# Seeds of a long convolution: phases that stay in PSUM, and sizes as eleven Exps on ScalarE

## The chip, the cores and the metric

One core of a Trainium2 chip runs the whole program. The metric is the device time of one execution in microseconds (us), the median of several runs. PE is the tensor engine (PEld its weight loads), DVE the vector engine, ACT the scalar engine, POOL the GpSimd engine, and SP issues the DMAs.

## The reference

Two independent blocks are written side by side into the output. Block B is softmax attention over 2048 positions with 16 heads of 28. Block A is a long convolution whose kernel is a sum of 256 complex exponentials for each of 448 channels:

```python
dt = jnp.exp(log_dt)
A = -jnp.exp(log_A_real) + 1j * A_imag
C = (C_real + 1j * C_imag) * dt[:, None]
P = jnp.exp((A * dt[:, None])[:, :, None] * pos[None, None, :])
K = 2.0 * jnp.einsum("dn,dnl->dl", C, P).real
y = irfft(rfft(u, 2L) * rfft(K, 2L))[:L] + u * D_skip
```

What matters here is P, the powers of z = exp(A dt) up to position 2047.

## The kernel before, in words

The kernel has two stages. The first projects x to q, k and v: 48 blocks of twelve matmuls each, in float32 split into a high and a low part, whose results leave PSUM through an ACT copy (the high part, hl or vst) and a DVE subtraction (the low part). PE has three PSUM tiles for these blocks, named pm. A block's hl goes to DRAM by a put on SP's queue, and the loads khat<-k and qhat<-q fetch it back. The first stage ends with the row maxima of the first 512 queries (mx, rl), which need those loads. The second stage runs attention and the convolution together, in a written order, up to the end.

The change is in the *seeds*, which run beside the projections. For eight groups of channels (seed 0 to 7), `seeds(o)` makes z to the powers 1, 2, 4, ..., 1024 (LV = 11 powers) for 112 exponents on each of 128 partitions, and from these the small tables that the second stage expands. Its steps are:

- `exp_a` and `times_dt` (ACT, nat): Exp of the decay parameters, and products with dt.
- `turn` (PE): eight transposes into the PSUM tile pn of the seed. Its part 0 is then the real part of A dt, part 1 the phase in turns, parts 2 and 3 are C.
- `phases` (DVE): reduces the phase to within half a turn in three small operations of 128x112 (round, subtract, clamp), and multiplies it with the eleven powers of two (pw) to r, 128x1232. On POOL it multiplies the real part with the same powers to mg, 128x1232.
- `reduce` (DVE): takes off whole turns, two operations of 128x1232.
- `sines` (ACT): sine, absolute value and cosine of 128x1232. `sizes` (ACT): Exp of mg, 128x1232.
- The rest (gz, sg, qhat, px on POOL, DVE and ACT) multiplies sizes with sines and cosines and puts the tables into DRAM. `fa`, `fb`, `e_base` and `g_base` read mg.

r, sn and mg are the three parts of one SBUF tile, tri, of which there are two. In groups of the profile "ACT tri<-tri" therefore holds sines, absolute values and the Exp of sizes alike; "DVE tri<-tri,pw" is the multiply of r, "DVE tri<-tri 128x112" the clamp, "POOL tri<-tr,pw" the product of mg, and tr is an SBUF copy of the real part that POOL reads.

Exp and Sin need different function tables on ACT; a change between them is an instruction of its own, ACT_TABLE_LOAD.

The steps of a seed are laid out over slots, four slots from one seed to the next, and the projections are spread evenly over 37 slots. In this stage a scheduler then orders each engine's queue by its own costs (in the second stage the written order is kept), and each engine works through its queue strictly in that order. All instructions pass through one helper, so the profile names line 75 for all of them; they are told apart by their tiles.

Of the kernel before, what the change touches and what calls it, by code (L numbers as in the profile page):

```python
# [2 lines left out]

# [5 lines left out]
F32 = mybir.dt.float32  # L9
F32R = mybir.dt.float32r  # L10
I32 = mybir.dt.int32
AF = mybir.ActivationFunctionType
ALU = mybir.AluOpType
# [42 lines left out]
LV = 11  # L56
# [4 lines left out]
MAGIC = 1.5 * 2 ** 23  # L61
TWO_PI = 6.283185
# [28 lines left out]
def body(ctx, tc, a, out):  # L91
# [5 lines left out]
    def pool(stack, name, bufs=1, space=None, side=None):  # L97
        kw = {} if space is None else {"space": space}
        if side:
            kw["side"] = side  # L100
        return stack.enter_context(tc.tile_pool(name=name, bufs=bufs, reuse_waits="tile", **kw))
# [110 lines left out]
    with ExitStack() as st:  # L212
        sst, xst, wst = ExitStack(), ExitStack(), ExitStack()
        t_p = pool(sst, "t_p")
        s_p = pool(sst, "s_p")
# [51 lines left out]
        half_pi = s_p.tile([128, 1], F32, name="half_pi")  # L267
# [42 lines left out]
        NH = BO * 16  # L310
        mul = lambda e, o_, x_, y_: e.tensor_tensor(o_, x_, y_, ALU.mult)

        def seeds(o):

            q = {}
            vec, pol, act = nc.vector, nc.gpsimd, nc.scalar
            lb = lambda v_: v_[:, None, :].to_broadcast([128, LV, NH])
            kb = pw2[:, :, None].to_broadcast([128, LV, NH])
            v = lambda t, k: t[:, k, :].rearrange("p (b h) -> p b h", h=16)
            vk = lambda t, k: t[:, k:k + 3, :].rearrange("p k (b h) -> p k b h", h=16)  # L320

            def exp_a():
                act.activation(q["nat"][:, 0, :], q["nat"][:, 0, :], AF.Exp)

            def times_dt(i):
                n, d = q["nat"][:, i, :], dt_all[:, i or 4, o:o + 1]
                act.activation(n, n, AF.Copy, scale=d)

            def turn():
                q["ps"] = ps = ps_n.tile([128, CQ], F32, name="pn")[:, :8 * PO].rearrange("p (a b h e) -> p a b h e", a=4, h=2, e=8)  # L330
                for i in range(4):
                    for h in range(2):
                        nc.tensor.transpose(ps[:, i, :, h, :], q["nat"][:, i, h * 128:(h + 1) * 128], ident[:PO, :PO])
                q["tr"] = s_p.tile([128, NH], F32, name="tr", bufs=2)
                act.activation(q["tr"], ps[:, 0].rearrange("p b h e -> p (b h e)"), AF.Copy)

            def phases():
                tri = t_p.tile([128, 3, LV, NH], F32, name="tri", bufs=2)
                q["r"], q["sn"], q["mg"] = r, sn, mg = tri[:, 0], tri[:, 1], tri[:, 2]
                t0, k0, im = sn[:, 0, :], sn[:, 1, :], q["ps"][:, 1].rearrange("p b h e -> p (b h e)")  # L340
                vec.tensor_scalar(k0, im, MAGIC, None, op0=ALU.add)
                vec.scalar_tensor_tensor(t0, k0, MAGIC, im, op0=ALU.subtract, op1=ALU.subtract)
                vec.tensor_scalar(t0, t0, 0.5, -0.5, op0=ALU.min, op1=ALU.max)
                mul(vec, r, lb(t0), kb)
                mul(pol, mg, lb(q["tr"]), kb)

            def reduce():
                vec.tensor_scalar(q["sn"], q["r"], MAGIC, MAGIC, op0=ALU.add, op1=ALU.subtract)
                vec.tensor_tensor(q["r"], q["sn"], q["r"], ALU.subtract)

            def sines():
                act.activation(q["sn"], q["r"], AF.Sin, scale=TWO_PI)
                act.activation(q["r"], q["r"], AF.Abs)
                act.activation(q["r"], q["r"], AF.Sin, scale=-TWO_PI, bias=half_pi)

            def sizes():
                act.activation(q["mg"], q["mg"], AF.Exp)

            def places():
                se = q_p.tile([128, HG, CQ], F32R, name="qhat", bufs=3).bitcast(F32).rearrange("p h q -> p (h q)")  # L360
# [40 lines left out]
            def factors(i, k, p_, n_):  # L401
                zz, mg = q["zz"], q["mg"]
                mul(vec, zz[:, i:i + 3, :, 0, :], vk(mg, k), vk(q["r"], k))
                mul(vec, zz[:, i:i + 3, :, p_, :], vk(mg, k), vk(q["sn"], k))
                for k in range(i, i + 3):
                    act.activation(zz[:, k, :, n_, :], zz[:, k, :, p_, :], AF.Copy, scale=-1.0)
# [20 lines left out]
            def load():  # L427
                if o not in nats:
                    load_nat(o)
                q["nat"] = nats.pop(o)  # L430
            dts = lambda *r: [lambda i=i: times_dt(i) for i in r]
            fa, fb = lambda: factors(0, 3, 2, 1), lambda: factors(3, 8, 1, 2)
            return [[load], [exp_a] + dts(1, 2, 3), dts(0), [turn], [phases], [reduce], [sines], [sizes, g_base],
                    [places, fa, e_base], [e3, g_first], [fb, e5, g_copies], [put_g], [put_e]]

        xh, xl = {}, {}
# [59 lines left out]
        for c in range(NQ):  # L496
# [4 lines left out]
            if c + 1 < NQ:  # L501
                jobs[1] = (lambda c, f: lambda: (load_x(c + 1), f())[1])(c, jobs[1])
            work += jobs
        stages = [seeds(o) for o in range(NO)]
        n_stage = SP * (NO - 1) + len(stages[0])
        slots = [[] for _ in range(n_stage)]
# [499 lines left out]
    for s in range(NS):  # L1006
# [25 lines left out]
        ps = []  # L1032
# [97 lines left out]
```

## Time and profile before

| | |
|---|---|
| timed runs | 1301.16, 1301.76, 1304.81 us; median 1301.76 |
| span of the profiled execution | 1301.1 us (1301.05 in the trace); its own device time is not listed apart from these runs |
| granted TensorE clock, mean | 0.978 |
| busy, share of the span | PE 94%, DVE 73%, ACT 73%, POOL 67% |

A group's line reads: line, engine, operation, output<-inputs, shape, count | busy us, mean ns | idle time of the engine just before, and what ended it. A piece of the chain of waits reads: start, length, what. A timeline line reads: start, length, engine, line, operation, tiles, shape, count, and in brackets the idle time before it. A row of a table of stretches has the busy time of PE, PEld, DVE, ACT and POOL, then the granted clock, the DMA engines' share and GB/s.

### The profile page before, as it was taken

What the parts mean: (1) busy time and instruction counts of PE and PEld (TensorE: products, weight loads), DVE (VectorE), ACT (ScalarE), POOL (GpSimd) and SP (SyncE); (2) the same over time, 40 slices, a digit from 0 to 9 for tenths busy, and PEclk for the clock granted to TensorE, in tenths of its full rate; (3) what the DMA queues carried; (4) which work ended last, traced back from release to release, by engine and by line L of the source; (5) the groups of instructions that cost most, each with busy time, mean ns of one, the idle gap of its engine ahead of it and who ended that gap; (6) DMA issues with size and microseconds to landing.
All of it is one profiled execution on the core that took longest, in us unless ns stands there. A gap on an engine that the chain in (4) does not pass through costs nothing.

```text
span 1301.1 us, 33177 instructions
## 1 busy us (share of the span) xinstructions
PE 1228.2 (94%) x12625; PEld 701.0 (54%) x12625; DVE 948.0 (73%) x2106; ACT 952.4 (73%) x2068; POOL 871.1 (67%) x736
## 2 busy tenths in 40 slices
PE   6878985899999999999999999999999999999997
PEld 5657763355555555555555555555555555544433
DVE  5887896987777887787788888888888655645111
ACT  4775763488888888888888888888887766756552
POOL 3676683298888878888869999998996212424421
PEclk9888997999999999999999999999999999999999
DMA  6677769835866555458644131733425453647656
GB/s 194 203 258 244 249 206 294 237 77 124 195 137 149 124 146 148 140 147 231 181 126 96 54 95 32 182 91 83 103 51 148 153 158 133 201 144 244 198 162 174
DMA packets 200088, 205.35 MB, mean 158 GB/s; under 512 B 95993, under 2 KB 158521, under 8 KB 197881
## 3 DMA queue, kind: packets, MB, share of 16 engines
q1 hardware_dynamic: 199928, 203.23, 56.2%
q8 instruction: 100, 1.64, 0.5%
q14 instruction: 60, 0.48, 0.1%
HBM read 120.73 MB, written 82.18 MB: 156 GB/s over the span
## 4 chain that ended last, share of the span: by engine, by line
PE 71%; DVE 10%; DMA 6%; POOL 5%; ACT 3%; issue 3%; SPq 0%; POOLq 0%; ACTq 0%; DVEq 0%
PE pm L75 40%; PE pss L75 16%; PE po L75 15%; DVE tri L75 2%; DVE mx L75 2%; POOL e L75 1%; POOL qhat L75 1%; DMA k<-hl 1%; ACT tri L75 1%; DVE qhat L75 1%; DVE sg L75 1%; DMA tri<-in_B_wqkv 1%; DVE px L75 1%; DMA khat<-k 1%; DMA ut<-in_A_u 1%
## 5 line engine op out<-in xcount | busy, mean ns | idle before, releaser
L75 ACT ACTIVATE p<-pss 128x512 f32<-128x512 f32 x1024 | 560.9, 609 | 111.6 <-PE pss L75 108.6
L75 PE MATMUL pss<-qhat,khat 128*128 128x512 f32 x1024 | 402.5, 399 | 1.5 <-ACT p L75 1.4
L75 DVE TENSOR_REDUCE mx<-pm 128x1 f32<-128x512 f32 x500 | 321.4, 684 | 109.2 <-PE pm L75 107.1
L75 PE MATMUL pm<-khat,qhat 128*128 128x512 f32 x749 | 326.3, 438 | 3.4 <-DVE mx L75 2.1
L75 POOL TENSOR_TENSOR e<-e,sdb 128x256 f32<-128x256 f32 x168 | 202.0, 1202 | 116.2 <-ACT e L75 61.2
L75 PE MATMUL po<-p,v 128*32 128x512 f32 x2048 | 269.1, 594 | 0.0
L75 POOL TENSOR_TENSOR e<-e,eu 128x256 f32<-128x256 f32 x168 | 248.4, 1478 | 13.2
L75 PEld LDWEIGHTS pm<-khat,qhat 128*128 128x128 f32 x749 | 141.0, 189 | 199.7 <-ACT p L75 47.8
L75 DVE CUSTOM_DVE_ANT_0 rl<-pm,rl 128x512 f32<-128x512 f32 x249 | 171.4, 688 | 65.2 <-ACT rl L75 61.5
L75 PEld LDWEIGHTS pss<-qhat,khat 128*128 128x128 f32 x1024 | 190.2, 188 | 45.7 <-issue 10.8
L75 POOL TENSOR_TENSOR eu<-e,sdb 128x256 f32<-128x256 f32 x168 | 202.2, 1203 | 0.0
L75 POOL TENSOR_TENSOR p<-pr,pr 64x448 f32<-64x448 f32 x64 | 73.3, 1145 | 158.5 <-PE pm L75 133.2
L75 ACT ACTIVATE rl<-pm 128x512 f32<-128x512 f32 x249 | 150.8, 606 | 20.4 <-PE pm L75 20.4
L75 DVE TENSOR_TENSOR g<-g,zg 128x128 f32<-128x128 f32 x392 | 162.1, 413 | 3.4
L75 PE MATMUL pm<-xh,khat 112*128 112x512 f32 x256 | 94.1, 451 | 23.2 <-DVE hl L75 11.1
L75 PE MATMUL pm<-kdif,qhat 128*128 128x512 f32 x249 | 100.5, 404 | 2.6 <-DMA v<-v 1.3
L75 DVE TENSOR_TENSOR zg<-g,zg 128x128 f32<-128x128 f32 x224 | 88.0, 393 | 5.0
L75 PEld LDWEIGHTS pm<-e,g 128*32 128x32 f32 x3584 | 57.2, 109 | 43.8 <-issue 16.1
L75 DVE TENSOR_TENSOR pr<-pm,ub 128x448 f32<-128x448 f32 x64 | 37.0, 619 | 56.4 <-PE pm L75 42.0
L75 PEld LDWEIGHTS pm<-xh,khat 112*128 112x128 f32 x256 | 54.2, 217 | 39.4 <-DVE hl L75 12.9
L75 PE MATMUL pm<-e,g 128*32 128x64 f32 x3584 | 73.0, 222 | 1.9 <-POOL e L75 1.9
L75 ACT ACTIVATE y<-pm 128x448 f32<-128x448 f32 x48 | 26.5, 553 | 58.2 <-PE pm L75 33.8
(134 smaller groups left out, 1470.3 us busy)
## 6 DMA issues: line engine op xcount, KB each, us to landing
sdb<-sd SPq DMA_DIRECT2D x56, 336.0 KB
khat<-k SPq DMA_DIRECT2D x64, 256.0 KB
qhat<-q SPq DMA_DIRECT2D x64, 256.0 KB
sd<-sg SPq DMA_DIRECT2D x8, 1456.0 KB
k<-hl SPq DMA_DIRECT2D x16, 512.0 KB
q<-hl SPq DMA_DIRECT2D x16, 512.0 KB
mw<-in_mw SPq DMA_DIRECT2D x16, 512.0 KB
sd<-qhat SPq DMA_DIRECT2D x8, 896.0 KB
```

The lines of the kernel that those rows point to most:

```text
L75: i = f(*args, **kw)
```

## The change

The copy tr and POOL's product are gone. The phase stays in PSUM through its three small operations (the first still writes its rounded copy to SBUF), and the multiply reads it from there. The sizes are eleven ACT instructions of 128x112, each Exp of the turned real part, read from PSUM, with the power of two as its scale. They stand right behind the phases in a seed's steps. A helper, `in_order`, tells the scheduler to keep those ACT steps that need a table (`exp_a`, `sizes`, `sines`) in the order in which they are written, over all seeds.

```diff
+        table = []
...
+            def in_order(f):
+                def call():
+                    with tc.issue_after(table[0]) if table else nullcontext():
+                        i = f()
+                    table[:] = [i.ins]
+                return call
...
-                q["tr"] = s_p.tile([128, NH], F32, name="tr", bufs=2)
-                act.activation(q["tr"], ps[:, 0].rearrange("p b h e -> p (b h e)"), AF.Copy)
...
-                t0, k0, im = sn[:, 0, :], sn[:, 1, :], q["ps"][:, 1].rearrange("p b h e -> p (b h e)")
-                vec.tensor_scalar(k0, im, MAGIC, None, op0=ALU.add)
-                vec.scalar_tensor_tensor(t0, k0, MAGIC, im, op0=ALU.subtract, op1=ALU.subtract)
+                k0, (tr, t0) = sn[:, 1, :], (q["ps"][:, i].rearrange("p b h e -> p (b h e)") for i in range(2))
+                vec.tensor_scalar(k0, t0, MAGIC, None, op0=ALU.add)
+                vec.scalar_tensor_tensor(t0, k0, MAGIC, t0, op0=ALU.subtract, op1=ALU.subtract)
                 vec.tensor_scalar(t0, t0, 0.5, -0.5, op0=ALU.min, op1=ALU.max)
                 mul(vec, r, lb(t0), kb)
-                mul(pol, mg, lb(q["tr"]), kb)
+                q["tr"] = tr
...
+            @in_order
+            def sizes():
+                return [act.activation(q["mg"][:, k, :], q["tr"], AF.Exp, scale=float(2 ** k)) for k in range(LV)][-1]
...
-            def sizes():
-                act.activation(q["mg"], q["mg"], AF.Exp)
...
-            return [[load], [exp_a] + dts(1, 2, 3), dts(0), [turn], [phases], [reduce], [sines], [sizes, g_base],
+            return [[load], [exp_a] + dts(1, 2, 3), dts(0), [turn], [phases, sizes], [reduce], [sines], [g_base],
```

More of the change, by code (lines that the diff above doesn't have):

```diff
@@ L1 @@
 import collections
-from contextlib import ExitStack
+from contextlib import ExitStack, nullcontext
 import concourse.bass as bass
@@ L320, in seeds @@
             vk = lambda t, k: t[:, k:k + 3, :].rearrange("p k (b h) -> p k b h", h=16)
+            def in_order(f):
[5 more added lines that the diff above has]
+            @in_order
             def exp_a():
-                act.activation(q["nat"][:, 0, :], q["nat"][:, 0, :], AF.Exp)
+                return act.activation(q["nat"][:, 0, :], q["nat"][:, 0, :], AF.Exp)
             def times_dt(i):
@@ L339, in phases @@
                 q["r"], q["sn"], q["mg"] = r, sn, mg = tri[:, 0], tri[:, 1], tri[:, 2]
-                t0, k0, im = sn[:, 0, :], sn[:, 1, :], q["ps"][:, 1].rearrange("p b h e -> p (b h e)")
-                vec.tensor_scalar(k0, im, MAGIC, None, op0=ALU.add)
-                vec.scalar_tensor_tensor(t0, k0, MAGIC, im, op0=ALU.subtract, op1=ALU.subtract)
+                k0, (tr, t0) = sn[:, 1, :], (q["ps"][:, i].rearrange("p b h e -> p (b h e)") for i in range(2))
+                vec.tensor_scalar(k0, t0, MAGIC, None, op0=ALU.add)
+                vec.scalar_tensor_tensor(t0, k0, MAGIC, t0, op0=ALU.subtract, op1=ALU.subtract)
                 vec.tensor_scalar(t0, t0, 0.5, -0.5, op0=ALU.min, op1=ALU.max)
                 mul(vec, r, lb(t0), kb)
-                mul(pol, mg, lb(q["tr"]), kb)
+                q["tr"] = tr
+            @in_order
+            def sizes():
+                return [act.activation(q["mg"][:, k, :], q["tr"], AF.Exp, scale=float(2 ** k)) for k in range(LV)][-1]
             def reduce():
@@ L349, in reduce @@
                 vec.tensor_tensor(q["r"], q["sn"], q["r"], ALU.subtract)
+            @in_order
             def sines():
@@ L353, in sines @@
                 act.activation(q["r"], q["r"], AF.Abs)
-                act.activation(q["r"], q["r"], AF.Sin, scale=-TWO_PI, bias=half_pi)
-            def sizes():
-                act.activation(q["mg"], q["mg"], AF.Exp)
+                return act.activation(q["r"], q["r"], AF.Sin, scale=-TWO_PI, bias=half_pi)
             def places():
```

## The prediction

> **What bounds the kernel now.** I read the page's chain of the whole span first, then a table of stretches, then the chain inside the stretch that the change touches.
>
> ```profile
> PE 71%; DVE 10%; DMA 6%; POOL 5%; ACT 3%; issue 3%; SPq 0%; POOLq 0%; ACTq 0%; DVEq 0%
> ```
>
> ```profile
> 28.00:191.00 163.00, 137.63 (x613) 111.04 (x611) 137.34 (x224) 116.86 (x232) 114.74 (x121) 0.91 0.70 235
> ...
> 196.60:215.00 18.40, 6.44 (x22) 4.85 (x20) 9.10 (x20) 4.75 (x10) 8.74 (x13) 0.69 1.04 294
> 216.00:247.00 31.00, 24.70 (x63) 11.72 (x61) 29.38 (x65) 9.24 (x16) 0.00 (x0) 0.93 1.00 288
> 260.00:1260.00 1000.00, 991.08 (x11443) 537.44 (x11442) 735.46 (x1707) 780.94 (x1732) 721.31 (x568) 1.00 0.51 136
> ```
>
> The columns are stretch, length, busy time of PE, PEld, DVE, ACT and POOL, granted clock, DMA share and GB/s. From 260 to 1260 us PE is busy for 991 of 1000 us, and the change has no instruction there. From 216 to 247 DVE's maxima are busy for 29.4 of 31 us. From 196.6 to 215 the DMA engines are full (1.04) with the loads that the maxima wait for. So whatever the change does to the seeds, between 28 and about 195 us, passes on to the end one for one: those three stretches only begin earlier or later. Within the seeds no engine is full: PE 137.6, DVE 137.3, ACT 116.9 and POOL 114.7 of 163 us. The limit there is a chain that changes engines, so I take its pieces (start, length, what):
>
> ```profile
> by line: DVE tri L75 16.8%; POOL qhat L75 10.7%; PE pm L75 10.3%; DVE sg L75 7.6%; DVE qhat L75 7.3%; ACT tri L75 6.6%; issue 6.5%; POOL tri L75 5.5%; DVE px L75 4.5%; DVE hl L75 3.7%; POOL x_e L75 2.9%; DMA sd<-qhat 2.5%; DMA v<-vst 2.2%;
> ...
> 46.92 1.77 DVE tri L75
> ...
> 77.07 3.41 POOL tri L75
> ...
> 116.00 6.54 PE pm L75 x24
> ...
> 124.41 1.98 DVE tri L75
> ...
> 143.78 2.96 DVE tri L75
> ...
> 160.97 2.28 DVE qhat L75
> ...
> 182.07 1.64 DVE tri L75
> ```
>
> DVE's work on tri (the phases) is the largest share, and POOL and DVE lines together hold more than half. The pieces of 1.6 to 3 us are the ones to explain, because the tiles in them are small.
>
> **What the change removes.** Groups, with count, busy time and mean ns:
>
> ```profile
> L75 ACT ACTIVATE tri<-tri 128x1232 f32<-128x1232 f32 x24 | 29.6, 1234 | 15.7 <-POOL tri L75 10.8 <-DVE tri L75 4.8
> L75 POOL TENSOR_TENSOR tri<-tr,pw 128x1232 f32<-128x1232 f32 x8 | 19.4, 2419 | 14.3 <-ACT tr L75 8.5 <-issue 5.8
> L75 ACT ACT_TABLE_LOAD x15 | 19.2, 1283 | 1.0 <-PEq L1120 0.7
> L75 DVE TENSOR_TENSOR tri<-tri,pw 128x1232 f32<-128x1232 f32 x8 | 15.1, 1886 | 0.1
> L75 DVE TENSOR_TENSOR hl<-pm,hl 128x512 fp32r<-128x512 f32 x16 | 11.0, 686 | 4.8 <-ACT hl L75 4.7
> L75 DVE TENSOR_TENSOR qhat<-qhat 128x112 f32<-128x112 f32 x16 | 10.1, 655 | 3.4 <-POOL qhat L75 3.4
> L75 DVE TENSOR_SCALAR tri<-tri 128x112 f32<-128x112 f32 x8 | 8.0, 1003 | 0.1
> L75 DVE TENSOR_TENSOR px<-pn,gz 128x224 f32<-128x224 f32 x16 | 6.4, 400 | 0.3
> L75 ACT ACTIVATE tr<-pn 128x112 f32<-128x112 f32 x8 | 2.2, 271 | 1.1 <-PE pn L75 0.9
> L75 DVE TENSOR_SCALAR tri<-pn 128x112 f32<-128x112 f32 x8 | 2.1, 267 | 0.2 <-ACT tr L75 0.2
> ```
>
> The clamp of the phases (tri<-tri, 128x112) takes 1003 ns on average, its neighbour from pn with as many elements 267. Two of its eight in order of time say why:
>
> ```profile
> 33.23 0.21 DVE L75 TENSOR_SCALAR tri<-tri 128x112 f32<-128x112 f32 x1
> ```
>
> ```profile
> 181.39 2.24 POOL L75 TENSOR_TENSOR tri<-tr,pw 128x1232 f32<-128x1232 f32 x1
> ...
> 181.95 1.76 DVE L75 TENSOR_SCALAR tri<-tri 128x112 f32<-128x112 f32 x1
> ```
>
> Alone it takes 0.21 us. At 181.95 it ends at 183.71, just as POOL's product does (183.63): DVE stood still behind POOL. The operations that have an operand in PSUM (hl, px) show nothing of the kind in their means.
>
> - *Clamp, in PSUM now.* The trace has no DVE instruction that writes PSUM of this size from PSUM. Its bounds are 0.21 and 1.00 us; I take the row from pn, 0.27. The three clamps on the chain give 1.50 + 1.71 + 1.37 = 4.6 us.
> - *Multiply to eleven powers, one operand in PSUM.* From 686 ns at 512 elements and 400 at 224, an element costs 0.99 ns, so 1232 take 1.40 us (bounds: that and today's 1.89). The one on the chain at 143.78 gives 2.96 - 1.40 = 1.6 us.
> - *POOL's product goes.* The multiply at 160.97 (qhat), held behind it, falls to its group's mean of 0.65: 1.6 us. At 77.07 it is itself on the chain. Late next there is DVE's multiply of the same seed:
>
> ```profile
> 76.08 2.29 DVE L75 TENSOR_TENSOR tri<-tri,pw 128x1232 f32<-128x1232 f32 x1
> ```
>
> ```profile
> 80.50 1.23 ACT L75 ACTIVATE tri<-tri 128x1232 f32<-128x1232 f32 x1 [2.79 <-POOL tri L75]
> ```
>
>   In the built program a seed's first Exp waits for that multiply, the last of DVE's four operations in the seed's PSUM tile. With 1.40 it ends at 77.48 instead of Exp's start at 80.50. That is 3.0 us earlier, less 0.7 by which the new Exps are longer (below): 2.3.
>
> Together 10.1 us of the chain. I count nine tenths, 9.0: paths beside it lie close, but they run over the same two engines, and off the chain DVE and POOL are released as well (eight clamps by 0.73 us, eight multiplies by 0.49, eight products of 2.42).
>
> **What it adds.** Eleven Exps of 128x112 from PSUM replace one of 128x1232 and the copy tr, in each of eight seeds. Bounds from rows: 11 x 0.271 = 2.98 us end to end, or overlapped as this row's six are:
>
> ```profile
> 195.35 1.22 ACT L75 ACTIVATE sg<-sg 128x112 f32<-128x112 f32 x6
> ```
>
> Six take 1.22, so one costs 0.20 us more and eleven some 0.27 + 10 x 0.18 = 2.0 (with 0.18 for the shorter single one). I take 2.0, nearest to the row that has them back to back. ACT gains 2.0 - 1.23 - 0.27 = 0.5 us a seed, 4 in all (12 by the other end). The order of the built program has 17 table loads in place of 15, another 2.6 us. So ACT gets 6.6 us more work and loses the 10.8 us that it waited for POOL's product. Bounds of what reaches the path: nothing, or all 6.6. ACT's tri is 6.6% of the chain, and only one Exp is on it, so I take a quarter: 1.6.
>
> [...]
>
> A table load is followed at once:
>
> ```profile
> 135.10 1.28 ACT L75 ACT_TABLE_LOAD   x1
> 136.40 0.42 ACT L75 ACTIVATE nat<-nat 56x256 f32<-56x256 f32 x1
> ```
>
> [...]
>
> **What it moves.** The last seed sets the tail, and there the order on ACT changes.
>
> ```profile
> 184.12 1.80 DVE L75 TENSOR_TENSOR tri<-tri,pw 128x1232 f32<-128x1232 f32 x1
> ...
> 190.76 1.23 ACT L75 ACTIVATE tri<-tri 128x1232 f32<-128x1232 f32 x1 [2.16 <-DVE tri L75]
> ...
> 194.00 0.69 DVE L75 TENSOR_TENSOR hl<-pm,hl 128x512 fp32r<-128x512 f32 x1 [0.57 <-ACT hl L75]
> ...
> 195.25 0.99 POOL L75 TENSOR_TENSOR tri<-tri 128x224 f32<-128x224 f32 x1 [2.20 <-ACT tri L75]
> ...
> 196.57 1.80 SPq L75 DMA_DIRECT2D khat<-k  x4
> ```
>
> Between sine and cosine stands the evacuation hl of a q block. Behind it wait PE for its PSUM tile and, on SP's queue, the put of q, then two loads of kdif, then khat<-k, which opens the full DMA stretch. Now hl ends 3.9 us after the sine starts. In the new order ACT does sine, absolute value and cosine first (3 x 1.23, as its tri group), two copies (0.27 each, as tr) and gz (0.4, as twice a copy's elements), 4.6 in all, and then hl; and DVE's half of hl stands behind an operation (0.4, as px) that waits for POOL's product of cosines: 4.6 + 0.1 + 1.0 + 0.4 + 0.7 = 6.8. So +2.9. From the multiply's end to the sine it is 190.76 - 185.92 = 4.8 now; then two table loads, Exps and an hl between them, 1.3 + 2.0 + 0.7 + 1.3 = 5.3: +0.5. Two px operations of seed 6 (0.4 each) go behind that multiply: -0.8. SP's own order from here on, and the bytes, are the same. The tail costs 2.6.
>
> **Sum:** -9.0 + 1.6 + 2.6 = -4.8. The profiled execution has a span of 1301.05 us; its own device time is not listed apart, and the timed runs start at 1301.16, so little lies around it. Against the span that is 1296.3; the median is 0.7 above it, which makes **1297.0**.
>
> **The rivals.**
>
> *The pair runs free (about 1292).* Everything that DVE loses counts: clamps 5.9, multiplies 3.9, the held qhat 1.6, and half of what the reductions lose today, 8 x (1.1 - 0.8) + 8 x (1.85 - 1.45):
>
> ```profile
> L75 DVE TENSOR_TENSOR tri<-tri 128x1232 f32<-128x1232 f32 x8 | 14.8, 1847 | 0.1
> ...
> L75 DVE TENSOR_SCALAR tri<-tri 128x1232 f32<-128x1232 f32 x8 | 8.8, 1098 | 0.1
> ```
>
> ```profile
> 127.89 0.81 DVE tri L75
> 128.72 1.45 DVE tri L75
> ```
>
> That is 14.2, so -14.2 + 1.6 + 2.6 = -10.0: 1291.8, and less where POOL's own 19.4 us count. For it: DVE and POOL hold the chain. Against: PE, ACT and the DMAs have stretches of their own in it.
>
> *The stall moves on (about 1301).* POOL keeps 95 of its 115 us, and now starts its other products earlier, beside DVE's reductions and sg products, which still have both operands in SBUF. Only the clamps' 4.6 are kept: -4.6 + 1.6 + 2.6 = -0.4, 1301.4. This is also the case in which the change does not do what it says.
>
> *The Exps hold up the evacuations (about 1312, slower).* The first Exp now waits at the head of ACT's queue for DVE's multiply; behind it stand the evacuations hl, vst and xh, and for these PE, which has three tiles: it can run two blocks, 6.54 us, before it stalls. The train is 1.28 + w + 2.0 + 0.42 (Exp of the next parameters) + 1.28 = 5.0 + w, so it decides from a wait w of 1.5 us on. The four waits for POOL's product averaged 10.8 / 4 = 2.7. With that in all eight seeds, and DVE's 0.7 for its half, PE loses 8 x 1.9 = 15 us: -4.8 + 15 = +10, 1312. Half of the seeds give 1304.5. Against: the wait is for an earlier operation than today's.
>
> **How the numbers follow.** A measurement of this kernel can tell about 0.3%, 3.9 us, from no change. I give the forecast (1293 to 1300) 0.45, the free pair 0.20, the moved stall 0.17 and the held evacuations 0.18. Faster by over 0.3% (below 1297.9): 0.31 of the forecast's 0.45 and the 0.20, 0.51. Within: 0.14 + 0.17 = 0.31. Slower: 0.18. The range 1289 to 1306 takes in the first three and the lower part of the last; 1293 to 1300 is the forecast's own.
>
> **What would show it.** Right: clamps near 0.27 us and multiplies near 1.4, ACT's wait for POOL tri gone, Exps about 0.18 us apart, the first khat<-k near 192, and all later stretches unchanged in length. Wrong: ACT waiting on DVE at the first Exps by more than 1.5 us each with PE's waits for hl rising above today's; clamps still near 1 us; or a shorter chain with khat<-k no earlier, which would put the error into the tail.

## The result, and the profile after

The changed kernel takes 1293.94 us, the median of four runs (1296.34, 1293.33, 1291.53, 1294.55), against 1303.28 of the kernel before beside it. The ratio is 0.9922, with a 95% interval of 0.9902 to 0.9942: 10.2 us faster (7.6 to 12.8). (The two medians differ by 9.3 us, which lies inside that interval; the expectations below name that figure.) The forecast was 4.8. The profiled execution is the slowest of the four: its span is 1294.3 us and its time 1296.34, so 2.0 us lie around the span. (The prediction took nearly nothing for that, for want of the number; the profiled execution of before then took some 1303.)

The chain of waits inside the seeds' stretch, 28 to 191 us, and then the table of stretches, both of the changed kernel. The two middle stretches are set 8 us earlier than those shown of before, as its loads and maxima begin earlier by that:

```profile
by line: PE pm L75 24.6%; ACT tri L75 11.4%; issue 7.4%; POOL qhat L75 6.6%; DVE tri L75 5.9%; DVE sg L75 5.6%; DVE qhat L75 4.9%; DMA q<-hl 3.8%; DVE px L75 3.7%; DVE hl L75 3.4%; POOL x_e L75 3.3%; POOL tri L75 3.0%; ACT L75 2.9%; PE pt L
```

```profile
28.00:191.00 163.00, 141.12 (x624) 115.20 (x624) 127.89 (x239) 129.83 (x322) 96.83 (x123) 0.88 0.72 245
...
188.50:207.00 18.50, 6.03 (x22) 4.49 (x20) 8.39 (x18) 2.83 (x7) 6.16 (x6) 0.68 1.04 292
...
208.00:239.00 31.00, 24.66 (x63) 11.59 (x61) 29.34 (x65) 9.30 (x16) 0.00 (x0) 0.94 1.01 287
260.00:1260.00 1000.00, 990.77 (x11448) 536.94 (x11446) 731.07 (x1697) 779.67 (x1730) 715.49 (x563) 1.00 0.51 137
```

In the chain of the seeds' stretch DVE's tri fell from 16.8% to 5.9%, and PE's pm, the projections, rose from 10.3% to 24.6%. The DMA stretch is as full as it was (1.04), the maxima as busy (29.3 of 31 us), and 260 to 1260 us unchanged. POOL has 18 us less work in the same 163 us, and ACT 13 more, in part because more of the stage falls into them (624 PE instructions for 613). The groups of the first 240 us:

```profile
L75 ACT ACT_TABLE_LOAD x17 | 21.8, 1283 | 4.8 <-DVE tri L75 3.9 <-PEq L1130 0.7
...
L75 DVE TENSOR_TENSOR sg<-tri 128x336 f32<-128x336 f32 x32 | 21.3, 680 | 10.5 <-ACT tri L75 10.5
...
L75 ACT ACTIVATE tri<-pn 128x112 f32<-128x112 f32 x88 | 15.2, 310 | 0.1
...
L75 DVE TENSOR_TENSOR tri<-tri 128x1232 f32<-128x1232 f32 x8 | 13.6, 1703 | 0.1
...
L75 DVE TENSOR_TENSOR tri<-pn,pw 128x1232 f32<-128x1232 f32 x8 | 11.4, 1429 | 0.0
...
L75 DVE TENSOR_TENSOR px<-qhat 128x112 f32<-128x112 f32 x16 | 8.5, 532 | 3.9 <-POOL qhat L75 3.7 <-issue 0.2
...
L75 DVE TENSOR_SCALAR tri<-tri 128x1232 f32<-128x1232 f32 x8 | 7.4, 930 | 0.0
L75 DVE TENSOR_TENSOR qhat<-qhat 128x112 f32<-128x112 f32 x16 | 7.2, 480 | 2.4 <-POOL qhat L75 2.4
...
L75 DVE TENSOR_SCALAR pn<-pn 128x112 f32<-128x112 f32 x8 | 2.2, 273 | 0.0
```

Clamps take 273 ns and multiplies 1429, as forecast (270 and 1400); the reductions and the qhat products became shorter too (1847, 1098 and 655 before); the products sg<-tri and px<-qhat hardly changed (684 and 504 before). ACT's waits of 10.8 us for POOL's product are gone; in their place a table load waited twice for DVE's multiply, 3.9 us in all.

The tail of the last seed, from the timeline, engine by engine:

```profile
171.30 1.42 DVE L75 TENSOR_TENSOR tri<-pn,pw 128x1232 f32<-128x1232 f32 x1
...
185.95 0.68 DVE L75 TENSOR_TENSOR hl<-pm,hl 128x512 fp32r<-128x512 f32 x1
```

```profile
174.09 1.83 ACT L75 ACTIVATE tri<-pn 128x112 f32<-128x112 f32 x11
...
177.80 1.23 ACT L75 ACTIVATE tri<-tri 128x1232 f32<-128x1232 f32 x1
...
182.85 0.39 ACT L75 ACTIVATE gz<-gz 128x224 f32<-128x224 f32 x1 [2.33 <-POOL gz L75]
...
184.36 0.57 ACT L75 ACTIVATE hl<-pm 128x512 fp32r<-128x512 f32 x1
```

```profile
188.50 1.98 SPq L75 DMA_DIRECT2D khat<-k  x4
```

The last seed's multiply ends at 172.72 (start and length) in place of 185.92: 13.2 us earlier. The first khat<-k is issued at 188.50 in place of 196.57, only 8.1 earlier. So the seeds gave more than forecast, and 5.1 us were given back between the two. Eleven Exps stand together in 1.83 us (forecast 2.0).

### The profile page after: what moved, and what is told of

Same layout as the page of the kernel before. It is cut to its first block, busy times and chain, and to the rows that moved or that the text cites. A ratio compares the mean times of both kernels' runs of the same rounds, so it can differ in the third digit from the quotient of the medians.

```text
span 1294.3 us, 33256 instructions
## 1 busy us (share of the span) xinstructions
PE 1228.1 (95%) x12625; PEld 703.1 (54%) x12625; DVE 933.2 (72%) x2106; ACT 956.6 (74%) x2142; POOL 847.0 (65%) x728
## 4 chain that ended last, share of the span: by engine, by line
PE 76%; DVE 9%; POOL 5%; ACT 4%; issue 3%; DMA 3%; SPq 0%; ACTq 0%; POOLq 0%; DVEq 0%
PE pm L75 43%; PE pss L75 16%; PE po L75 16%; DVE mx L75 2%; ACT tri L75 1%; POOL e L75 1%; DVE rl L75 1%; DMA khat<-k 1%; POOL qhat L75 1%; DVE tri L75 1%; DVE px L75 1%; DVE sg L75 1%; DVE qhat L75 1%; POOL p L75 1%; PE pt L75 1%
## 5 line engine op out<-in xcount | busy, mean ns | idle before, releaser
L75 POOL TENSOR_TENSOR e<-e,eu 128x256 f32<-128x256 f32 x168 | 248.1, 1477 | 13.2
L75 PEld LDWEIGHTS pss<-qhat,khat 128*128 128x128 f32 x1024 | 190.7, 189 | 45.7 <-issue 10.8
L75 PE MATMUL pm<-xh,khat 112*128 112x512 f32 x256 | 90.3, 434 | 14.1 <-DVE hl L75 7.1
```

The source lines that it names most:

```text
L75: i = f(*args, **kw)
```

## The experiments

Two theories stood against each other. *Release*: the gain is DVE and POOL set free, by PSUM operands that POOL doesn't hold (before, 267 ns for the rounding from pn and 1003 for the clamp in SBUF, of the same shape) and by the product that is gone. *Order*: the gain comes from the new order of ACT's functions, and the edits matter little. A scheduler orders this stage anew after every edit, so beside the ratio I read three points of each profiled execution: the end of the last seed's multiply, the first khat<-k, and the first copy rl of the maxima. *Tail* is from the first to the second, *loads* from the second to the third. The end follows the third within 3.8 us (span less first rl: 1085.4 to 1089.2 in all fourteen).

| kernel | multiply ends | tail | loads | span | ratio to before (95%) |
|---|---|---|---|---|---|
| before | 185.92 | 10.65 | 19.11 | 1301.1 | |
| after | 172.72 | 15.78 | 19.24 | 1294.3 | 0.9922 (0.9902 to 0.9942) |
| e1 phases in PSUM alone | 181.52 | 15.13 | 19.61 | 1302.0 | 1.0008 (0.9995 to 1.0022) |
| e2 Exps on ACT alone | 171.24 | 15.70 | 19.48 | 1292.5 | 0.9938 (0.9922 to 0.9953) |
| e3 changed, free order | 167.82 | 11.47 | 19.19 | 1286.5 | 0.9875 (0.9857 to 0.9893) |
| e4 new order alone | 186.27 | 15.86 | 19.18 | 1307.4 | 1.0049 (1.0033 to 1.0066) |
| e5 changed, product back | 179.18 | 15.76 | 19.43 | 1300.8 | 0.9993 (0.9983 to 1.0004) |
| e17 as e2, product back | 186.76 | 15.73 | 19.39 | 1310.7 | 1.0055 (1.0043 to 1.0068) |
| e16 changed, hl ahead | 169.32 | 13.64 | 19.55 | 1289.0 | 0.9908 (0.9893 to 0.9923) |
| e10 as e2, free order | 167.41 | 18.97 | 19.29 | 1292.8 | 0.9925 (0.9912 to 0.9937) |
| e18 changed, hl behind sine | 169.74 | 12.47 | 15.54 | 1286.9 | 0.9876 (0.9861 to 0.9891) |
| e19 as e1, hl behind sine | 183.72 | 12.53 | 15.99 | 1299.1 | 0.9966 (0.9952 to 0.9979) |
| e20 as e10, hl behind sine | 167.19 | 18.50 | 15.70 | 1289.2 | 0.9889 (0.9873 to 0.9906) |
| e8 changed, Exps twice | 182.49 | 11.36 | 19.13 | 1300.4 | 0.9983 (0.9975 to 0.9991) |

Each run of a batch was timed beside the kernel before on its chip. Differences between ratios below are given in us of 1304 (the median of before in the three batches was 1304.2 to 1304.75), with the two intervals added as squares.

### Halves and order (e1 to e4)

e1 starts from the kernel before:

```diff
-                t0, k0, im = sn[:, 0, :], sn[:, 1, :], q["ps"][:, 1].rearrange("p b h e -> p (b h e)")
-                vec.tensor_scalar(k0, im, MAGIC, None, op0=ALU.add)
-                vec.scalar_tensor_tensor(t0, k0, MAGIC, im, op0=ALU.subtract, op1=ALU.subtract)
+                k0, t0 = sn[:, 1, :], q["ps"][:, 1].rearrange("p b h e -> p (b h e)")
+                vec.tensor_scalar(k0, t0, MAGIC, None, op0=ALU.add)
+                vec.scalar_tensor_tensor(t0, k0, MAGIC, t0, op0=ALU.subtract, op1=ALU.subtract)
```

> Only the first half: phases stay in PSUM; the copy tr, POOL's product and the one Exp of 128x1232 stay as in the kernel before, and so does the free order of the functions (15 table loads). Release theory (DVE is freed where an operand is in PSUM, and POOL's product is a cost of its own): clamps 0.27 us and multiplies 1.4 us, ACT's wait for POOL tri still about 10 us, and 4 to 6 us of the 9.3 that the whole change gained, 1297 to 1299. If this half is all of it: 1294. Order theory (the gain is that of the new order of ACT's functions): no gain, 1302 to 1304.

e2 is the changed kernel with t0 in sn again (the diff of e1 turned round). e3 is the changed kernel without its three `@in_order`:

```diff
-            @in_order
             def sizes():
```

e4 is the kernel before with `in_order` on its three steps, and sizes moved behind the phases in the list of steps:

```diff
+            @in_order
             def sizes():
-                act.activation(q["mg"], q["mg"], AF.Exp)
+                return act.activation(q["mg"], q["mg"], AF.Exp)
...
-            return [[load], [exp_a] + dts(1, 2, 3), dts(0), [turn], [phases], [reduce], [sines], [sizes, g_base],
+            return [[load], [exp_a] + dts(1, 2, 3), dts(0), [turn], [phases, sizes], [reduce], [sines], [g_base],
```

> Only the second half: eleven Exps from PSUM and no product on POOL, in the new order, but the phases in SBUF as before. Release theory: the clamps were held behind just the product that is gone, so most of them fall to 0.2 to 0.4 us with operands in SBUF too, and the mean goes below 0.6; multiplies 1.4 to 1.9; total 1295 to 1298. If the place of the operands is what counts: clamps stay near 1.0, because POOL's other products take the place of the one removed, total 1299 to 1301. Order theory: 1294, whatever the clamps do.

> The changed kernel with the order of ACT's functions left free; 19 table loads in place of 17. Release theory: the gain stays but for the two loads, 2.6 us of ACT's time of which at most all is seen: 1294 to 1297. Order theory: the gain is gone, 1302 to 1304.

> The kernel before with the new order alone: the Exp of the powers is written right behind the phases and the functions keep that order (17 table loads in place of 15); phases in SBUF, POOL's product, one Exp of 128x1232. Release theory: no gain, and the two loads and the earlier wait for POOL's product cost up to some 5 us: 1303 to 1308. Order theory: 1294 to 1296.

The order theory falls: without the order the change gives 16.3 us in place of 10.2, and the order alone costs 6.4 (plus or minus 2.2), somewhat more than the 5 that the release theory allowed. Nearly all of that cost is in the tail: the multiply ends at 186.27 in e4 and at 185.92 before, the tail is 15.86 in place of 10.65.

In e1 the clamps and multiplies were as short as in the changed kernel:

```profile
L75 DVE TENSOR_TENSOR tri<-pn,pw 128x1232 f32<-128x1232 f32 x8 | 11.5, 1438 | 0.2
...
L75 DVE TENSOR_SCALAR pn<-pn 128x112 f32<-128x112 f32 x8 | 2.2, 272 | 0.1
```

The last multiply ended 4.4 us earlier, but nothing was left of it in the time. In e1's order ACT's evacuation hl stands behind the cosine, a table load and six copies sg, and the tail took 4.5 back:

```profile
189.18 1.29 ACT L75 ACTIVATE tri<-tri,half_pi 128x1232 f32<-128x1232 f32 x1
...
193.49 0.58 ACT L75 ACTIVATE hl<-pm 128x512 fp32r<-128x512 f32 x1
```

The time is the one that the order theory named (no gain), but not for its reason, and the release theory's 4 to 6 us did not arrive. e3, in turn, gained more than the release theory allowed (1287.92 for 1294 to 1297): its free order has hl directly behind the last sine, and a tail of 11.47.

e2 has no PSUM operands for the phases, and yet DVE is free:

```profile
L75 DVE TENSOR_TENSOR tri<-tri,pw 128x1232 f32<-128x1232 f32 x8 | 11.6, 1455 | 0.1
...
L75 DVE TENSOR_SCALAR tri<-tri 128x112 f32<-128x112 f32 x8 | 2.3, 283 | 0.1
```

283 ns a clamp and 1455 a multiply, where they had 1003 and 1886 before, and a time of 1296.13 us: as the release theory expected. So it was above all the one product of POOL, issued at the same moment, that held them (before, the three longest clamps, 1.77, 1.97 and 1.76 us, stood beside it, two more, of 0.86 and 1.02, beside a product x_e<-qhat), and once it is gone the place of the operands matters little: e2 and the changed kernel differ by 2.1 us, plus or minus 3.3.

### The product put back (e5 and e17)

```diff
-                k0, (tr, t0) = sn[:, 1, :], (q["ps"][:, i].rearrange("p b h e -> p (b h e)") for i in range(2))
+                k0, (tr, t0) = s_p.tile([128, NH], F32, name="k0", bufs=2), (q["ps"][:, i].rearrange("p b h e -> p (b h e)") for i in range(2))
...
+                junk = s_p.tile([128, LV, NH], mybir.dt.bfloat16, name="junk")
+                mul(pol, junk, lb(k0), kb)
```

Nothing reads junk. k0 gets a tile of its own, which the product reads. e5 is the changed kernel with this, e17 is e2 with it. In both kernels each queue is as in its twin (after, e2) but for these eight products, so that the scheduler has no part in the difference.

> The changed kernel with POOL's product of eleven powers put back, written to a tile that nothing reads (in 16 bits, for room), so that no engine waits for it; every engine's order is that of the changed kernel but for these eight instructions. Theory A (the product costs by POOL's time and by what it holds on DVE): clamps stay at 0.27 us as their operands are in PSUM, but reductions and qhat products on DVE get longer again and POOL's 19 us delay what follows; 5 us or more of the gain are lost, a ratio to the kernel before of 0.996 to 1.001. Theory B (the product cost by ACT's wait for it at the one Exp): nobody waits now, the ratio stays at 0.992 to 0.994.

> The run with the phases in SBUF and the Exps on ACT, with POOL's product put back in the same way, read by nobody; every engine's order is that of that run but for the eight products. Clamps should go back from 0.28 to some 1.0 us, held behind the product. Theory A: ratio to the kernel before 0.999 to 1.004, and the step from its twin without the product is larger than that of the pair with the phases in PSUM by 2 to 5 us, since here the clamps and multiplies are held too. Theory B: 0.994 to 0.996, though the clamps are long.

```profile
L75 DVE TENSOR_TENSOR sg<-tri 128x336 f32<-128x336 f32 x32 | 23.9, 759 | 10.1 <-ACT tri L75 10.1
...
L75 POOL TENSOR_TENSOR junk<-k,pw 128x1232 bf16<-128x1232 f32 x8 | 18.5, 2315 | 7.4 <-DVE k L75 7.4
...
L75 DVE TENSOR_TENSOR tri<-tri 128x1232 f32<-128x1232 f32 x8 | 14.8, 1854 | 0.1
...
L75 DVE TENSOR_TENSOR tri<-pn,pw 128x1232 f32<-128x1232 f32 x8 | 11.4, 1431 | 0.1
...
L75 DVE TENSOR_TENSOR px<-qhat 128x112 f32<-128x112 f32 x16 | 10.3, 646 | 4.0 <-POOL qhat L75 3.7 <-ACT sg L75 0.3
...
L75 DVE TENSOR_TENSOR qhat<-qhat 128x112 f32<-128x112 f32 x16 | 8.7, 574 | 2.2 <-POOL qhat L75 2.2
...
L75 DVE TENSOR_SCALAR tri<-tri 128x1232 f32<-128x1232 f32 x8 | 7.7, 962 | 0.0
...
L75 DVE TENSOR_SCALAR pn<-pn 128x112 f32<-128x112 f32 x8 | 2.2, 272 | 0.0
```

```profile
L75 DVE TENSOR_TENSOR tri<-tri,pw 128x1232 f32<-128x1232 f32 x8 | 16.0, 2001 | 0.1
...
L75 DVE TENSOR_SCALAR tri<-tri 128x112 f32<-128x112 f32 x8 | 10.3, 1283 | 0.1
```

Theory A holds in both (e17 lies a little above its range). The product that nobody waits for costs 9.3 us (plus or minus 2.9) with the phases in PSUM, nearly all that the change gained, and 15.3 (2.6) with them in SBUF. In e5 clamps (272) and multiplies (1431) are untouched by it, but the product now holds what stands beside them, DVE work that still has its operands in SBUF. In seed 3, e5 has, on POOL and on DVE,

```profile
96.34 2.25 POOL L75 TENSOR_TENSOR junk<-k,pw 128x1232 bf16<-128x1232 f32 x1 [0.25 <-DVE k L75]
```

```profile
96.65 2.18 DVE L75 TENSOR_TENSOR px<-qhat 128x112 f32<-128x112 f32 x1
```

and the changed kernel, for the same instruction,

```profile
96.63 0.37 DVE L75 TENSOR_TENSOR px<-qhat 128x112 f32<-128x112 f32 x1
```

That is 1.8 us, and the multiply of that seed ends 1.85 us later (100.64 for 98.79). Over all seeds sg<-tri, px<-qhat, the qhat products and the reductions get longer by 7.3 us: (759 - 680) x 32 + (646 - 532 + 574 - 480) x 16 + (1854 - 1703 + 962 - 930) x 8 ns. In e17 clamps (1283) and multiplies (2001) are held for 12.4 us more than in e2, sg<-tri (786 for 703) for 2.7 more, and px<-qhat (573 for 614) for 0.7 less: 14.4 in all. So 7.1 us more of holding cost some 6.0 (3.9) more, and the holding on DVE, 7.3 and 14.4 us, is nearly the whole of the two prices, 9.3 and 15.3. What is left for POOL's own time, 18.5 us ahead of the tables in its queue and 7.4 us in which it stands there waiting for k, is 2.0 and 0.9 us, not told from nothing. No run separates the two, and none shows that each us of holding reaches the end: in e1, which has another order, clamps, multiplies and these groups together are 10.1 us shorter than before the change, and the last multiply ends only 4.4 earlier.

Beside the same product the multiply takes 1431 ns with one operand in PSUM (e5) and 2001 with both in SBUF (e17), and px<-qhat above, with both in SBUF, 2.18 us in place of 0.37. By what POOL holds DVE, no run here shows.

### The tail (e16, e18, e19) and the free order (e10, e20)

e16 holds the last seed's absolute value, gz and cosine, and its negated factors, behind ACT's hl of the q block:

```diff
+                    hls.append(nc.scalar.activation(th, pp, AF.Copy).ins)
...
+                mark[:] = [hls[-2]]
+                with tc.issue_after(mark[0]):
+                    act.activation(q["r"], q["r"], AF.Abs)
```

> The changed kernel, in which the last seed's absolute value, gz and cosine are put behind ACT's evacuation hl of the q block (and so is DVE's half, two places earlier); the order of PE, POOL and SP is that of the changed kernel. Tail theory (the 5 us between the last multiply and the first khat<-k that the changed kernel gives back are ACT's order there): DVE's hl ends about 3 to 4 us earlier, first khat<-k near 185, ratio to the kernel before 0.989 to 0.990. Rival (the tail waits for something else, POOL's products or SP): khat<-k no earlier than 188, ratio 0.992.

The tail fell by 2.1 us in place of 3 to 4, and the ratio by 1.8 us (plus or minus 3.3, so not told from none). hl still waited, as the copies sg<-px of the seed before stood ahead of it, and these waited 3.27 us for DVE:

```profile
179.37 0.56 ACT L75 ACTIVATE sg<-px 128x112 f32<-128x112 f32 x2 [3.27 <-DVE sg L75]
179.73 0.63 ACT L75 ACTIVATE hl<-pm 128x512 fp32r<-128x512 f32 x1
```

e18 puts these copies behind hl as well. For that seed 6's `g_copies` and `put_g` had to be written later, which moved one more thing, its put sd<-sg on SP's queue, behind two loads qhat<-q and four khat<-k:

```diff
-                    [places, fa, e_base], [e3, g_first], [fb, e5, g_copies], [put_g], [put_e]]
+                    [places, fa, e_base], [e3, g_first], [fb, e5] + [g_copies] * (o != NO - 2),
+                    [put_g] * (o != NO - 2), ([g_copies, put_g] if o == NO - 2 else []) + [put_e]]
```

e19 and e20 make the same edit in e1 and in e10 (e10 is e2 without `@in_order`). In e16, e18, e19 and e20 the queues are those of their twins up to the last sine, but for two copies sg<-pn that e20 moves from before that sine to behind the cosine.

> The changed kernel with ACT's evacuation hl of the last q block directly behind the last seed's sine; absolute value, gz, cosine and the copies sg of the seed before come after it, and DVE's half is two places earlier than in the changed kernel. All else is in the order of the changed kernel. Tail theory: from the last multiply's end to the first khat<-k 12 to 13 us in place of 15.8, as DVE's half now waits for DVE's own queue alone; ratio to the kernel before 0.989 to 0.990. Rival (something else holds the tail): 15 us or more, ratio 0.991 to 0.993.

> The run with phases in PSUM alone, with the same tail as the last one: hl directly behind the last sine; the order before that is unchanged. If that run's 4.4 us at the last multiply were real and only the tail's order ate them: tail 11 to 13 us in place of 15.1, ratio to the kernel before 0.997 to 0.998 from 1.0008, 4 us faster than the kernel before. Rival (released clamps and multiplies are worth nothing, as the timed run says): 1.000 to 1.001.

> Exps on ACT in a free order of ACT's functions, phases in SBUF: the run with the free order without the first half of the change. If the place of the phases is worth the 2 us by which the two runs in the new order differ: ratio to the kernel before 0.989 to 0.990. If the product was all that held the clamps and the place is worth nothing: 0.987 to 0.988, with clamps near 0.28 us.

> The run in the free order with the phases in SBUF, with the same tail: hl directly behind the last sine, the order before that unchanged. Its tail of 19.0 us should fall to 11 to 13. If the place of the phases is worth nothing once POOL's product is gone: ratio to the kernel before 0.987 to 0.988, as the free order with the phases in PSUM. If it is worth the 6 us by which the two free orders differ: it stays at 0.990 to 0.9925.

e18 from ACT, DVE and SP:

```profile
174.82 1.23 ACT L75 ACTIVATE tri<-tri 128x1232 f32<-128x1232 f32 x1
176.18 0.60 ACT L75 ACTIVATE hl<-pm 128x512 fp32r<-128x512 f32 x1
```

```profile
179.65 0.68 DVE L75 TENSOR_TENSOR hl<-pm,hl 128x512 fp32r<-128x512 f32 x1
```

```profile
182.21 1.98 SPq L75 DMA_DIRECT2D khat<-k  x4
...
190.25 2.13 SPq L75 DMA_DIRECT2D khat<-k  x4
...
194.22 0.38 SPq L75 DMA_DIRECT2D sd<-sg  x1
```

hl follows the sine at once, the tail is 12.47 us, and the first khat<-k starts at 182.21. DVE's half ends at 180.33, since it stands behind seed 6's work in DVE's queue. The ratio beat the expectation (0.9876 for 0.989), and the table says why: the loads take 15.54 us in place of 19.24, with the put sd<-sg issued at 194.22, behind the second khat<-k. In the changed kernel it went ahead of that one and of two loads qhat<-q:

```profile
193.43 0.56 SPq L75 DMA_DIRECT2D sd<-sg  x1
...
195.85 3.51 SPq L75 DMA_DIRECT2D khat<-k  x4
```

```profile
sd<-sg SPq DMA_DIRECT2D x1, 1456.0 KB
```

A put of 1456 KB into DMA engines that are full for the whole stretch: 1.456 MB at the 292 GB/s of the stretch's row are 5.0 us, and the loads, which the maxima wait for, end 3.6 to 3.7 us earlier without it (19.24 to 15.54, 19.61 to 15.99, 19.29 to 15.70). e16, which leaves the put where it was, keeps 19.55. So e18's 6.0 us (plus or minus 3.3) are two edits: 3.3 of the tail and 3.7 of the loads by the traces. In e19 it is 2.6 and 3.6, timed 5.5 (2.5). Its expectation was all but met in the ratio (0.9966 for 0.997 to 0.998) and met in the tail (12.53), not in the reason: the last multiply ends only 2.2 us before that of the kernel before, and of its 4.4 us about 1 would be left without the put.

e20 misses. Its tail stays (18.50 for 18.97), because hl there waits for the DMA of the q<-hl before it:

```profile
181.76 0.60 ACT L75 ACTIVATE hl<-pm 128x512 fp32r<-128x512 f32 x1 [4.58 <-DMA q<-hl]
```

The 4.7 us (2.7) that it gained on e10 are the loads' 3.6. Both expectations for e10 miss too (0.9925): its tail is the longest of all. Its clamps take 367 ns, not 283: two of the eight, with operands in SBUF, are still long (0.98 and 0.68 us), though POOL's product of eleven powers is gone. The two kernels still tell what the place of the phases is worth in the free order: the last multiply ends at 167.41 and 167.19 with the phases in SBUF, and at 167.82 with them in PSUM, so nothing up to there that single executions could show. The 6.5 us (2.9) between e10 and e3 are the tail's 7.5.

### What ACT's added work costs (e8)

```diff
-                return [act.activation(q["mg"][:, k, :], q["tr"], AF.Exp, scale=float(2 ** k)) for k in range(LV)][-1]
+                return [act.activation(q["mg"][:, k, :], q["tr"], AF.Exp, scale=float(2 ** k)) for _ in range(2) for k in range(LV)][-1]
```

> The changed kernel with each seed's eleven Exps done twice over, the same values written again: 14.6 us more of ACT's work (8 x 1.83). The order of all engines shifts with it, so that some us of noise must be allowed for. If a quarter of ACT's work reaches the end, as the forecast had it: 3.7 us slower than the changed kernel, ratio to the kernel before 0.994 to 0.996. If ACT has room for it: 0.991 to 0.993. If all of it counts: 1.002 to 1.005.

```profile
L75 ACT ACTIVATE tri<-pn 128x112 f32<-128x112 f32 x176 | 29.4, 364 | 0.3 <-DVE tri L75 0.2
```

14.2 us more of Exps (29.4 for 15.2) made the kernel 8.0 us slower (plus or minus 2.8): more than half. In the trace the last multiply is 9.8 us later than in the changed kernel, of which the tail, in another order, gave 4.4 back. None of the three expectations has it; the quarter is too little, and all of it too much. As the order of all engines is another in e8, no closer price can be read from it: with the tail of the changed kernel 12.4 of the 14.2 us would have counted (8.0 + 4.4, an estimate).

## Why the prediction was right, and where its sum was wrong

The direction and the mechanism were right: POOL's product held DVE and ACT, and the change released them (clamps from 1003 to 273 ns, ACT's 10.8 us of waiting gone). The sum of -4.8 was half of what came, because the product's term was far too small; the costs on ACT and in the tail were too small as well, and the PSUM operands were counted beside the product that had held them. That the time fell into 1293 to 1300 all the same, 0.9 us above its fast end, was in part luck: gain and costs were both underrated, and the sum was put on a span that lies some 2 us below the device time.

- *What bounds the kernel; all passes on one for one.* Right: the loads kept their length in all rows of the table but e18, e19 and e20, where a put was moved, and what comes after them in all rows.
- *Clamp and multiply in PSUM, 4.6 + 1.6.* Durations right (273 and 1429 ns). At the last multiply these two are worth 4.4 and 2.2 us as long as the product runs (e1, e19), 7.6 in the new order (e5 against e17, 8.1 in time, plus or minus 2.1), and nothing that can be measured once it is gone (e2, e10, e20). In the prediction they were added to the product's removal, though the removal alone sets them free.
- *POOL's product goes, 1.6 + 2.3.* The step that failed. It took the pieces in which the product lies on one execution's chain; put back unread, it cost 9.3, of which DVE's holding can be 7.3, at sg<-tri, px<-qhat, qhat and the reductions. The loss is not at two places but collects along the seeds: the ends of the multiplies of e5 and of the changed kernel stand 34.11 and 34.05 in seed 0, 100.64 and 98.79 in seed 3, 141.75 and 138.26 in seed 5, 179.18 and 172.72 in seed 7. (Against e16 and e18, without the lower clock that the last section shows in the profile of the changed kernel, seed 7's differ by 9.9 and 9.4.)
- *Together -9.0.* Measured 13.2 at the last multiply, with ACT's added work already in it; e16 and e18, whose queues are the same up to there, ended at 169.32 and 169.74, 16 us and more ahead of before.
- *What it adds, +1.6.* The Exps' 2.0 us (measured 1.83) and the 17 loads were right, and a load is followed at once, as the prediction held (0.01 to 0.02 us behind it, for 16 of the 17). The quarter was too small: by e8 (8.0 of 14.2) the 5.8 us that ACT's busy time rose in the first 240 us (147.47 to 153.27) would be some 3.3, an estimate.
- *What it moves, +2.6 (3.4 behind the multiply).* The right place, and too small: the tail took 5.1. From the multiply's end to the sine it was 5.08 (forecast 5.3). From the sine to the end of DVE's hl it was 8.83 in place of 6.8, since gz was priced at its 0.4 us alone: ACT waited 2.33 us for POOL's gz, which stands on POOL behind seed 6's products.
- *The rivals.* "The pair runs free" had nearly the measured gain (-10.0 for -10.2), and its terms came nearly as it had them: from before to after the clamps lost 5.8 us, the multiplies 3.7, qhat 2.8 and the reductions 2.5, 14.8 in all for its 14.2. By e5 and e17 most of what DVE is held does count, so this rival was nearer to the cause than the forecast; that its sum met the time so closely is luck, as it had the forecast's costs, and of these the tail alone was 2.5 us too small. "The stall moves on" falls for the change: reductions became shorter (1847 to 1703 ns); it does move on where the product stays (e5). "The Exps hold up the evacuations" falls as a price of waiting: the wait of more than 1.5 us that it needs in all eight seeds came twice (3.9 us together, the longest 2.2).
- *What would show it.* As said there, but for the first khat<-k, at 188.5 in place of 192.

Taken as a path, from before over e1 and e5 to after, the last multiply moves by -4.4, -2.3 and -6.5 us, and the tail by +4.5, +0.6 and 0.0. The first step is the PSUM operands; the second is ACT, which no longer waits for the product, has eleven Exps for one and keeps the written order; the third is the product itself. So the wait that went about paid for ACT's added work; in time that step is 2.0 us (plus or minus 2.2), not told from none. These are single executions, and two of one order differ by 3 us at the last multiply; the account doesn't close better than that.

The best two versions are e3, the change without its forced order, and e18, the change with hl behind the sine and the put behind the loads: 0.9875 and 0.9876, some 16 us faster than the kernel before and 6 (plus or minus 3.5) than the changed one. Both fixes together were not tried.

## What to carry to other kernels

An engine's work that nobody waits for can still cost time, by what it holds on another engine while it runs: here it held DVE instructions with their operands in SBUF that came beside it (clamps of 1283 ns in e17, 283 in e2, and multiplies of 2001, 1455 in e2), and taking these two out of its way left others to be held (in e5 a px<-qhat of 2.18 us, 0.37 in the changed kernel). Price its removal by all that it holds in every round, not by the pieces of one chain; compare every group of the held engine before and after, not only those that the edit touches; and test it by putting it back unread with every queue left as it was. Release terms that have one cause must not be added: ask first whether removing the holder alone already frees what the second edit protects. Where a scheduler sets the order, read a gain at the point where the edit ends and again at the first transfer behind it, and look there for the evacuation and the large put that stand in the wrong place.

## What the hardware showed beside

The granted clock differs between executions with the same queues. The changed kernel and e18 have the same queues up to the last sine, and PE the same gap of 2.4 us before the rows below; then the changed kernel goes on at a lower clock (0.50 from 34.0 to 40.5 us, 1.00 until 33.8), and a pair of matmuls takes 1.05 us until 40.9, in place of 0.63 from the second pair on:

```profile
34.44 1.22 PE L75 MATMUL pm<-xh,khat 112*128 112x512 f32 x2 [2.39 <-DVE kb L75]
...
35.89 1.05 PE L75 MATMUL pm<-xh,khat 112*128 112x512 f32 x2
...
40.90 0.63 PE L75 MATMUL pm<-xh,khat 112*128 112x512 f32 x2
```

```profile
33.90 0.73 PE L75 MATMUL pm<-xh,khat 112*128 112x512 f32 x2 [2.38 <-DVE kb L75]
...
34.70 0.63 PE L75 MATMUL pm<-xh,khat 112*128 112x512 f32 x2
```

The granted clock of the stretch from 36 to 56 us, behind the five busy times of its row, is 0.88 in the changed kernel and 1.00 in e18:

```profile
36.00:56.00 20.00, 20.00 (x89) 17.02 (x88) 15.04 (x30) 15.05 (x35) 12.64 (x17) 0.88 0.66 225
```

```profile
36.00:56.00 20.00, 18.75 (x95) 15.57 (x94) 15.96 (x32) 15.63 (x37) 12.44 (x16) 1.00 0.67 226
```

Seed 0's multiply, which starts ahead of the lower clock (32.61 in the changed kernel), ends at 34.05 in the one and at 33.51 in the other, seed 1's at 58.18 and 56.46, seed 7's at 172.72 and 169.74. So the clock fell in the same gap of 2.4 us in the one execution and not in the other; no run here shows why.

Eleven activations of 128x112 from PSUM back to back are 1.83 us (the changed kernel), 22 are 3.55 (e8): 0.16 us for each of the second eleven, below the 0.18 taken from six copies in SBUF.
